# Both products with v of a round side by side, the scores laid out anew over five PSUM banks

## The chip, the cores and the metric

One Trainium2 chip, one of its cores. The metric is the device time of one execution in microseconds, as the median of several runs. A profile of one further execution gives the span from the first to the last instruction.

## What is computed

A gate mixes two branches over the same x (2048 positions, 640 features): a Fourier mix A and an attention B with 32 heads of 20 features that share one k and one v.

```python
g = sigmoid((x * gate_w).sum(-1, keepdims=True))
# A: a = x @ hid_re.T ; b = x @ hid_im.T ; y = seq_re @ a - seq_im @ b
# B: q = x @ wq per head ; k = x @ wk ; v = x @ wv
#    o = softmax(q k^T * 20**-0.5) v ; B = o @ wo
out = g * A + (1 - g) * B
```

All is float32. The large products use a float32r high part and a low part, three products for one.

## The kernel before

The first 266 us make q, k, v and the gate, then a and b of the Fourier branch. From there on a long stage runs two streams interleaved on TensorE (PE), which an order written out by hand sets: for ScalarE, VectorE, GpSimd and PE the instructions run as the program issues them.

*Attention.* The heads are taken in 16 pairs. Head 0 of a pair lies in partitions 0 to 63 and head 1 in 64 to 127, so a score product fills one half of PE's rows and two of them, one on each half, run beside each other. There are two kinds of scores. A unit `a` (`a_unit`, L319) multiplies a block of 128 queries by 512 keys and VectorE reduces it to its row maximum (L326). It works some 12 units ahead, mostly for the pair to come. A unit `b` (`b_unit`, L647) multiplies 128 keys by 512 queries, with the maximum in two extra rows, and ScalarE writes the exponential to an SBUF tile `pt` (L655). The products with v (`av_step`, L659) take four `pt` tiles, 128 keys deep, and write four groups of 32 columns of one bank: 128x32 tiles of PE, plain float32. Sixteen of them add up in a bank, and `finish_half` copies it out.

*Fourier.* The products `y` (L551) fill half of PE's rows as well, 320 columns wide, with one accumulating bank for each half (F0, F1). `y_evict` has ScalarE copy them out once 48 products a half are through.

A **round** issues 12 y on each half, 4 b and 4 a for each head, and two V, each an `av_step` on tiles of the round before. The string `ROUND` is its order, and `ROUND_LAST` that of the last pair's 16 rounds, which have no a. In these strings `y0` is a y on half 0, `a1S0` a score a of head 1 into bank S0, `b0S2` a score b of head 0 into bank S2, `V` an `av_step`, `E0` an eviction of y. Eight PSUM banks serve it: F0 and F1 for y, one bank V for the products with v, and S0 to S4 for the scores. A bank takes its next score when VectorE or ScalarE has read the last one; PE's weight load for that score carries the wait.

The last pair's products with v are laid out otherwise before: `av_half` splits the 128 keys into two halves of PE's rows (64x32 tiles, L676), `W0` and `W1` in the order, into two banks, V and S4; `finish_half` copies both (L691, L692) and GpSimd adds them (L693). After the 16 pairs 32 groups of products with wo (`o_group`, L114 to L116) end the kernel, and behind the first of them the last products with v run.

`clock` and `tick` count pairs of a (of b in the last pair). `a_reduce` (L332) runs one tick after a pair's last a, `a_final` (L340) three, and `finish_sums` (L716) 24 ticks after a pair's sums are out.

Of the kernel before, what the change touches and what calls it, by code (L numbers as in the profile page):

```python
# [8 lines left out]
F32 = mybir.dt.float32  # L9
F32R = mybir.dt.float32r  # L10
AF = mybir.ActivationFunctionType
ALU = mybir.AluOpType
# [5 lines left out]
P = 128  # L18
# [5 lines left out]
NT = S // P  # L24
NPAIR = H // 2
LAST = NPAIR - 1
# [3 lines left out]
ROW = 512  # L30
# [3 lines left out]
def kernel(  # L34
# [13 lines left out]
    nc = tc.nc  # L48
# [43 lines left out]
    vsb = const.tile([P, NT, 32], F32, name="vsb")  # L92
# [12 lines left out]
    def move(dst, src):  # L105
        nc.sync.dma_start(words(dst), words(src))  # L106
# [13 lines left out]
    RG = (slice(0, P // 2), slice(P // 2, P))  # L120
# [247 lines left out]
    def a_half(hh, tag="A"):  # L368
        u = state[hh]
        if u >= NA:  # L370
            return
        a_unit(u, hh, tag)
        state[hh] = u + 1
        if state[1 - hh] <= u:
            return
        if u % 64 == 16 and u // 64 + 1 < NPAIR:
            load_qs(u // 64 + 1)
        if u % 64 == 63:
            later(1, a_reduce, u // 64)
            later(3, a_final, u // 64)  # L380
# [35 lines left out]
    for it, t in enumerate(T2):  # L416
        load_x2(it + 2)
        j = t % SJ
# [37 lines left out]
    op = ctx.enter_context(tc.tile_pool(name="op", bufs=2))  # L456
# [113 lines left out]
    def y_evict(g):  # L570

        if not ended:
            return
        grp = ended[0]
        if "t" not in grp:
            grp["t"] = [op.tile([P, HALF], F32, name=n) for n in ("yt", "yu")]
            grp["left"] = 2
        y_half(g, grp["t"], grp["tb"], grp["ps"])
        grp["left"] -= 1
        if grp["left"] == 0:  # L580
            ended.pop(0)
            y_sum(grp["sh"], grp["tb"], grp["e"], grp["t"], grp["y0"])
# [53 lines left out]
    def y_put(n):  # L636

        while n > 0:
            n -= next(ys)[1]

    av = {}
    pt = {}

    def b_unit(p, hh, kc, qc, tag="B"):
        b = 64 * hh
        ps = bank(tag, f"b_{p}_{kc}_{qc}_{hh}")
        nc.tensor.matmul(  # L647
            ps,
            ks[b : b + 62, kc * P : (kc + 1) * P],
            qs[p][b : b + 62, qc * ROW : (qc + 1) * ROW],  # L650
            start=True,
            stop=True,
        )
        t = pp.tile([P, ROW], F32, name="pt")
        nc.scalar.activation(t, ps, AF.Exp, scale=SCALE)  # L655
        pt[(hh, kc, qc)] = [t, 2 if p == LAST else 1]

    def av_mm(ps, g, t, kc, first, last):
        nc.tensor.matmul(ps[32 * g : 32 * g + 32, :], vsb[:, kc, :], t, start=first, stop=last)  # L659

    def av_step(p, qh, kc):
        if kc == 0:
            av[qh] = bank("V", f"av_{p}_{qh}")
        for hh in range(2):
            for j in range(2):
                av_mm(av[qh], 2 * hh + j, pt.pop((hh, kc, 2 * qh + j))[0], kc, kc == 0, kc == NT - 1)

    avh = {}

    def av_half(g, p, qh, kc):  # L670

        if kc == 0:
            avh[g] = bank(("V", "S4")[g], f"av_{p}_{qh}_{g}")
        for i in range(4):
            key = (i // 2, kc, 2 * qh + i % 2)
            nc.tensor.matmul(  # L676
                avh[g][32 * i : 32 * i + 32],
                vsb[RG[g], kc, :],
                pt[key][0][RG[g]],
                start=kc == 0,  # L680
                stop=kc == NT - 1,
            )
            pt[key][1] -= 1
            if pt[key][1] == 0:
                pt.pop(key)

    def finish_half(p, qh):
        ob = op.tile([P, ROW], F32, name="ob")
        if p == LAST:
            oc = op.tile([P, ROW], F32, name="oc")  # L690
            nc.scalar.activation(ob, avh[0], AF.Copy)  # L691
            nc.scalar.activation(oc, avh[1], AF.Copy)  # L692
            nc.gpsimd.tensor_tensor(ob, ob, oc, op=ALU.add)  # L693
        else:
            nc.scalar.activation(ob, av[qh], AF.Copy)
        for hh in range(2):
            h = 2 * p + hh
            for j in range(2):
                js = slice((2 * qh + j) * ROW, (2 * qh + j + 1) * ROW)
                g = 32 * (2 * hh + j)  # L700
                move(sum_d[h : h + 1, js], ob[g + DH : g + DH + 1])
                move(oT_d[h * DH : (h + 1) * DH, js], ob[g : g + DH])
        if p == LAST:
            sm = op.tile([P, 16], F32, name="sm")
            ts = slice(qh * S // 2, (qh + 1) * S // 2)
            for hh in range(2):
                move(sm[64 * hh : 64 * hh + 64], sum_d[2 * p + hh, ts].rearrange("(s t) -> s t", t=16))
            later(4, finish_last, ts, sm)
        elif qh == 1:
# [14 lines left out]
    def finish_last(ts, sm):  # L724
# [10 lines left out]


    ROUND = (
        "y0 y1 y0 a1S0 b0S2 y1 b1S3 y0 y0 y1 y0 y1 y0 a1S1 y0 b0S4 y1 y1 y0 y1 y0 y1 y0 y1 "
        "a0S2 y1 y1 b0S3 a1S0 y0 y0 y1 b1S1 E1 a0S4 V a0S3 a1S0 E0 b0S1 b1S2 V b1S1 a0S4"
    ).split()  # L740

    ROUND_LAST = (
        "b1S3 y0 y1 y1 y0 y1 y0 b0S1 y1 y1 y0 b1S2 y0 y0 y1 y1 y0 y0 y1 y0 y1 y1 y0 b0S3 b1S0  "
        "y1 y0 y1 E1 y0 E0 b1S1 b0S2 W0 W1 W0 W1 b0S0"
    ).split()
    YR = ROUND.count("y0")
    ROUNDS = [(p, qh, kk) for p in range(NPAIR) for qh in range(2) for kk in range(NT // 2)]
# [5 lines left out]
        7: (lambda: [load_y(tb) for tb in range(4)],),  # L753
    }
    old = []
    old_h = [[], []]

    def av_next(g):
        if old_h[g]:
            st = old_h[g].pop(0)  # L760
            av_half(g, *st)
            if st[2] == NT - 1 and st not in old_h[1 - g]:
                finish_half(*st[:2])

    for rnd in ROUNDS:
        p, qh, kk = rnd
        nb, na, fed = [0, 0], 0, False
        new = [(p, qh, 2 * kk), (p, qh, 2 * kk + 1)]
        plan = ROUND
        if p == LAST:  # L770
            plan = ROUND_LAST

            if rnd[1:] == (0, 0):
                plan = ["V" if w == "W0" else w for w in plan if w != "W1"]
        for what in plan:
            if what == "V":
                if old:
                    st = old.pop(0)
                    av_step(*st)
                    if st[2] == NT - 1:  # L780
                        finish_half(*st[:2])
                continue
            g = int(what[1])
            if what[0] == "y":
                if not fed:
                    y_put(YR)
                    fed = True
                halves.run(g)
            elif what[0] == "E":
                y_evict(g)  # L790
            elif what[0] == "W":
                av_next(g)
            elif what[0] == "b":
                b_unit(p, g, 2 * kk + nb[g] // 2, 2 * qh + nb[g] % 2, what[2:])
                if p == LAST and sum(nb) % 2 == 0:
                    tick()
                nb[g] += 1
            else:
                if na % 2 == 0:
                    tick()  # L800
                a_half(g, what[2:])
                na += 1
        if p < LAST:
            old += new
        for g in range(2):
            old_h[g] += new if p == LAST else []
        if p == LAST and qh == 1:
            for f in BEFORE.get(kk, ()):
                f()
# [6 lines left out]
    for i in range(2 * NT):  # L816
        tb, e = divmod(i, 2)
        o_group(tb, e)
        tick()
        if i == 0:  # L820
            for g in (0, 1, 0, 1):
                av_next(g)
        n, k = divmod(i, 4)
        if k == 1:
            mult_o(n + 2)
        elif k == 2:
            split_o(n + 2)
            load_o(n + 3 if n else NO)
        if e == 1:
            load_y(tb + 4)  # L830
# [47 lines left out]
```

## Time and profile before

| | |
|---|---|
| time, median of 3 runs | 1862.59 us (1862.51 to 1863.89) |
| the profiled execution, span of its instructions | 1860.4 us |
| PE, weight loads, VectorE, ScalarE, GpSimd busy | 99%, 66%, 78%, 68%, 21% of the span |
| scores a and b, 512 columns | 2048 of each |
| y products, 320 columns | 6144 |
| records of products with v | 3840 (L659) and 512 (L676) |
| HBM traffic | 82 GB/s over the span |

Each float32 product with v shows as two records, so an `av_step` is eight records and two V of a round are sixteen. In a timeline's row stand the start in us from the span's start, the duration, the engine (PEld is the loading of weights on PE), the line, the operation, its tiles and shape, and how many records were merged; in brackets the idle time of the engine ahead of it and what ended that. In the list of waits the columns are the total in us, how often, and the longest.

### The profile page before, as it was taken

How to read it: one execution, taken by the hardware profiler on the slowest of the kernel's cores; microseconds unless marked ns; L12 is line 12 of the kernel's file. 1: busy time of each engine (PE TensorE's matmuls, PEld its weight loads, DVE VectorE, ACT ScalarE, POOL GpSimd, SP SyncE). 2: the span in 40 equal slices, each digit the busy share in tenths (PEclk: the TensorE clock that was granted, in tenths of full speed). 3: DMA queues.
4: the chain of work that ended last, by engine and by line, in shares of the span. 5: the costliest groups of instructions: out<-in, count | busy, mean ns of one | idle time of the engine just before them, and what ended most of it. 6: DMA issues, size and time to landing. Idle time of an engine off the chain costs nothing.

```text
span 1860.4 us, 42326 instructions
## 1 busy us (share of the span) xinstructions
PE 1846.3 (99%) x17368; PEld 1228.9 (66%) x17368; DVE 1449.3 (78%) x2307; ACT 1269.3 (68%) x2425; POOL 391.9 (21%) x336
## 2 busy tenths in 40 slices
PE   8999999999999999999999999999999999999999
PEld 6799986566566656656655665665566566566689
DVE  4469988888888888888888888888888888883144
ACT  4333357777777777777777777777777777778830
POOL 0033431111111111111111222222222212221132
PEclk9999999999999999999999999999999999999999
DMA  7684111211112021212114412121212121111366
GB/s 246 180 262 169 42 37 41 58 42 49 51 33 67 26 61 30 57 33 63 37 56 156 172 50 64 49 65 49 64 49 61 46 65 49 44 49 39 94 203 231
DMA packets 89023, 150.64 MB, mean 81 GB/s; under 512 B 21620, under 2 KB 58484, under 8 KB 86308
## 3 DMA queue, kind: packets, MB, share of 16 engines
q1 hardware_dynamic: 88828, 147.93, 25.8%
q8 instruction: 136, 2.23, 0.5%
q14 instruction: 59, 0.48, 0.1%
HBM read 103.91 MB, written 48.23 MB: 82 GB/s over the span
## 4 chain that ended last, share of the span: by engine, by line
PE 96%; DMA 2%; SPq 1%; DVE 1%; ACT 0%; issue 0%; POOL 0%; ACTq 0%; DVEq 0%
PE av L659 26%; PE y L551 23%; PE b L647 16%; PE a L319 16%; PE ab L125 7%; PE av L676 2%; PE o L114 1%; PE o L116 1%; PE o L115 1%; SPq L106 1%; PE q L116 1%; PE q L114 1%; PE q L115 0%; DMA ql_d<-ql 0%; DMA wraw<-in_wiT_dram 0%; DMA wraw<-in_wrT_dram 0%
## 5 line engine op out<-in xcount | busy, mean ns | idle before, releaser
L326 DVE TENSOR_REDUCE mx<-a 128x1 f32<-128x512 f32 x2048 | 1316.3, 686 | 217.1 <-PE a L319 124.3
L655 ACT ACTIVATE pt<-b 128x512 f32<-128x512 f32 x2048 | 1099.7, 599 | 358.6 <-PE b L647 352.5
L319 PE MATMUL a<-ks,qs 60*128 60x512 f32 x2048 | 755.8, 430 | 0.2 <-ACT pt L655 0.2
L551 PE MATMUL y<-ab,ch 64*128 64x320 f32 x4096 | 688.2, 307 | 1.2 <-DVE both L441 1.2
L647 PE MATMUL b<-qs,ks 62*128 62x512 f32 x2048 | 685.2, 407 | 0.7 <-ACT pt L655 0.7
L551 PEld LDWEIGHTS y<-ab,ch 64*128 64x128 f32 x4096 | 569.5, 186 | 12.8 <-DVE both L441 1.5
L659 PE MATMUL av<-pt,vsb 128*32 128x512 f32 x3840 | 511.3, 605 | 0.0
L647 PEld LDWEIGHTS b<-qs,ks 62*128 62x128 f32 x2048 | 331.8, 187 | 219.0 <-ACT pt L655 218.2
L319 PEld LDWEIGHTS a<-ks,qs 60*128 60x128 f32 x2048 | 335.0, 184 | 198.9 <-ACT pt L655 198.2
L551 PE MATMUL y<-ab,cl 64*128 64x320 f32 x2048 | 456.0, 308 | 0.0
L551 PEld LDWEIGHTS y<-ab,cl 64*128 64x128 f32 x2048 | 347.1, 187 | 0.8
L659 PEld LDWEIGHTS av<-pt,vsb 128*32 128x32 f32 x3840 | 76.0, 108 | 154.8 <-issue 146.5
L561 POOL TENSOR_TENSOR yt<-yt,yu 128x320 f32<-128x320 f32 x64 | 56.8, 888 | 575.6 <-ACT yt L556 563.2
L397 POOL CAST ch<-craw 128x1024 fp32r<-128x1024 f32 x62 | 64.4, 1039 | 477.1 <-PE a L319 441.3
L398 POOL TENSOR_TENSOR cl<-craw,ch 128x1024 fp32r<-128x1024 f32 x62 | 147.7, 2383 | 5.0
L125 PE MATMUL ab<-wh,xh 64*128 64x320 f32 x640 | 134.6, 308 | 1.5 <-DVE gz L235 1.1
L125 PE MATMUL ab<-wl,xh 64*128 64x320 f32 x640 | 134.1, 306 | 0.0
L125 PE MATMUL ab<-wh,xl 64*128 64x320 f32 x640 | 133.8, 306 | 0.0
L410 POOL TENSOR_TENSOR ab<-both,ab 128x320 fp32r<-128x320 f32 x64 | 60.3, 948 | 189.5 <-DMA craw<-in_cre_dram 99.9
L125 PEld LDWEIGHTS ab<-wh,xl 64*128 64x128 f32 x640 | 96.4, 185 | 0.0
L125 PEld LDWEIGHTS ab<-wl,xh 64*128 64x128 f32 x640 | 96.2, 185 | 0.0
L440 ACT ACTIVATE half<-ab 128x320 f32<-128x320 f32 x64 | 28.0, 437 | 88.4 <-PE ab L125 88.4
(86 smaller groups left out, 967.3 us busy)
## 6 DMA issues: line engine op xcount, KB each, us to landing
craw<-in_cre_dram SPq DMA_DIRECT2D x32, 512.0 KB
craw<-in_cim_dram SPq DMA_DIRECT2D x32, 512.0 KB
qs<-qh_d SPq DMA_DIRECT2D x64, 160.0 KB
ab_d<-ab SPq DMA_DIRECT2D x16, 640.0 KB
y_d<-yt SPq DMA_DIRECT2D x64, 160.0 KB
ab<-ab_d SPq DMA_DIRECT2D x16, 640.0 KB
xr<-in_xT_dram SPq DMA_DIRECT2D x20, 256.0 KB
xr<-in_xT_dram SPq DMA_DIRECT2D x16, 320.0 KB
```

The source lines that it names most:

```text
L114: nc.tensor.matmul(ps, wh, xh, start=(i == 0), stop=False)
L125: nc.tensor.matmul(ps, w[r], x[r], start=(i == 0 and k == 0), stop=(i == n - 1 and k == 2))
L319: nc.tensor.matmul(ps, qs[p][b : b + 60, qb * P : (qb + 1) * P], ks[b : b + 60, c * ROW : (c + 1) * ROW], start=True, stop=True,)
L326: nc.vector.tensor_reduce(mx[p][:, hh, qb, c : c + 1], ps, axis=AX.X, op=ALU.max)
L397: eng.tensor_copy(h, raw)
L398: eng.tensor_tensor(l, raw, h.bitcast(F32), op=ALU.subtract)
L410: nc.gpsimd.tensor_tensor(lo, both, hi.bitcast(F32), op=ALU.subtract)
L551: nc.tensor.matmul(ps, w, x, start=start, stop=stop)
L561: nc.gpsimd.tensor_tensor(yt, yt, yu, op=ALU.add)
L647: nc.tensor.matmul(ps, ks[b : b + 62, kc * P : (kc + 1) * P], qs[p][b : b + 62, qc * ROW : (qc + 1) * ROW], start=True, stop=True,)
L655: nc.scalar.activation(t, ps, AF.Exp, scale=SCALE)
L659: nc.tensor.matmul(ps[32 * g : 32 * g + 32, :], vsb[:, kc, :], t, start=first, stop=last)
```

## The change

`ROUND` and `ROUND_LAST` are written anew: the two V of a round stand side by side at its end, and y, a and b and their banks are spread otherwise. The counts of y, a, b, V and E in a round stay as they are, and so do each bank's (S0, S2, S3, S4 three times, S1 four times). The last pair uses `av_step` like the others; `av_half`, its second bank and the addition go away.

```diff
-        pt[(hh, kc, qc)] = [t, 2 if p == LAST else 1]
+        pt[(hh, kc, qc)] = t
...
-    def av_half(g, p, qh, kc):
...
     def finish_half(p, qh):
         ob = op.tile([P, ROW], F32, name="ob")
-        if p == LAST:
-            oc = op.tile([P, ROW], F32, name="oc")
-            nc.scalar.activation(ob, avh[0], AF.Copy)
-            nc.scalar.activation(oc, avh[1], AF.Copy)
-            nc.gpsimd.tensor_tensor(ob, ob, oc, op=ALU.add)
-        else:
-            nc.scalar.activation(ob, av[qh], AF.Copy)
+        nc.scalar.activation(ob, av[qh], AF.Copy)
...
     ROUND = (
-        "y0 y1 y0 a1S0 b0S2 y1 b1S3 y0 y0 y1 y0 y1 y0 a1S1 y0 b0S4 y1 y1 y0 y1 y0 y1 y0 y1 "
-        "a0S2 y1 y1 b0S3 a1S0 y0 y0 y1 b1S1 E1 a0S4 V a0S3 a1S0 E0 b0S1 b1S2 V b1S1 a0S4"
+        "a0S1 b1S0 b1S3 y0 y0 a1S2 y0 y1 y0 y1 b0S4 b1S0 a0S1 y1 y0 y1 y0 y1 y0 a1S3 b0S2 y0 y1 y0 y1 "
+        "a0S1 b1S4 y1 y0 y1 b0S0 y1 y0 y1 a1S2 y0 b0S3 y1 a1S4 a0S1 E0 E1 V V"
     ).split()
     ROUND_LAST = (
-        "b1S3 y0 y1 y1 y0 y1 y0 b0S1 y1 y1 y0 b1S2 y0 y0 y1 y1 y0 y0 y1 y0 y1 y1 y0 b0S3 b1S0  "
-        "y1 y0 y1 E1 y0 E0 b1S1 b0S2 W0 W1 W0 W1 b0S0"
+        "b1S3 b0S2 b1S0 y0 y0 y1 b0S4 y1 y1 y0 y1 y0 y1 b0S1 y1 y0 b1S3 y0 y1 y0 y1 y0 y1 y0 y1 y0 "
+        "y1 y0 y1 y0 b1S2 b0S0 E0 E1 V V"
     ).split()
...
-        if p < LAST:
-            old += new
-        for g in range(2):
-            old_h[g] += new if p == LAST else []
+        old += new
...
         if i == 0:
-            for g in (0, 1, 0, 1):
-                av_next(g)
+            for st in old:
+                av_step(*st)
+            finish_half(*old[-1][:2])
```

What PE gets at the end of a middle round before, in the order of issue. In these names `a_0_...` is a score a of head 0 with a running number, `b_11_3_0_...` a score b of key block 11, query block 3, head 0; `x4` is one V.

```order
L319 MATMUL a_0_5211<-ks,qs_867 128x512
L659 MATMUL av_1_4834<-pt,vsb 32x512 x4
L319 MATMUL a_0_5218<-ks,qs_867 128x512
L319 MATMUL a_1_5221<-ks,qs_867 128x512
L647 MATMUL b_11_3_0_5224<-qs_865,ks 128x512
L647 MATMUL b_11_2_1_5228<-qs_865,ks 128x512
L659 MATMUL av_1_4834<-pt,vsb 32x512 x4
L647 MATMUL b_11_3_1_5236<-qs_865,ks 128x512
L319 MATMUL a_0_5240<-ks,qs_867 128x512
```

Four scores stand between the two V, two for each head. On PE at the same place now:

```order
L319 MATMUL a_1_5323<-ks,qs_867 128x512
L319 MATMUL a_0_5326<-ks,qs_867 128x512
L659 MATMUL av_1_4855<-pt,vsb 32x512 x8
L319 MATMUL a_0_5337<-ks,qs_867 128x512
L647 MATMUL b_14_2_1_5340<-qs_865,ks 128x512
```

Both V have become one run of eight; the scores that stood between them have moved into the rest of the round. On PE, what follows directly in the new order:

```order
L647 MATMUL b_14_3_1_5344<-qs_865,ks 128x512
L551 MATMUL y_1_1_0_5063<-ab_3153,ch 128x320 x2
L319 MATMUL a_1_5350<-ks,qs_867 128x512
L551 MATMUL y_1_1_0_5063<-ab_3153,cl 128x320
L551 MATMUL y_1_1_1_5064<-ab_3153,ch 128x320
L551 MATMUL y_1_1_0_5063<-ab_3346,ch 128x320
L551 MATMUL y_1_1_1_5064<-ab_3153,ch 128x320
L647 MATMUL b_14_2_0_5357<-qs_865,ks 128x512
L647 MATMUL b_15_2_1_5361<-qs_865,ks 128x512
L319 MATMUL a_0_5365<-ks,qs_867 128x512
```

The last row, `a_0_5365`, uses bank S1 again, which `a_0_5337` behind the V used, and `b_15_2_1_5361` uses S0 again after `b_14_2_1_5340`. In the last pair, PE's order at the end of a round before:

```order
L647 MATMUL b_1_3_1_27305<-qs_865,ks 128x512
L647 MATMUL b_1_2_0_27309<-qs_865,ks 128x512
L676 MATMUL av_0_0_26768<-pt,vsb 32x512 x4
L676 MATMUL av_0_1_26773<-pt,vsb 32x512 x4
L676 MATMUL av_0_0_26768<-pt,vsb 32x512 x4
L676 MATMUL av_0_1_26773<-pt,vsb 32x512 x4
L647 MATMUL b_1_3_0_27345<-qs_865,ks 128x512
L647 MATMUL b_2_2_1_27349<-qs_865,ks 128x512
```

And PE's order at the end of a round of the last pair now:

```order
L647 MATMUL b_11_1_1_27038<-qs_865,ks 128x512
L647 MATMUL b_11_1_0_27042<-qs_865,ks 128x512
L659 MATMUL av_0_26772<-pt,vsb 32x512 x8
L647 MATMUL b_12_0_1_27054<-qs_865,ks 128x512
L647 MATMUL b_12_0_0_27058<-qs_865,ks 128x512
```

The round's last b of head 0 has moved from behind the products with v to the place ahead of them.

More of the change, by code (lines that the diff above doesn't have):

```diff
@@ L665, in av_step @@
             for j in range(2):
-                av_mm(av[qh], 2 * hh + j, pt.pop((hh, kc, 2 * qh + j))[0], kc, kc == 0, kc == NT - 1)
-    avh = {}
-    def av_half(g, p, qh, kc):
[L672 to L685, printed above, removed]
+                av_mm(av[qh], 2 * hh + j, pt.pop((hh, kc, 2 * qh + j)), kc, kc == 0, kc == NT - 1)
     def finish_half(p, qh):
         ob = op.tile([P, ROW], F32, name="ob")
-        if p == LAST:
-            oc = op.tile([P, ROW], F32, name="oc")
-            nc.scalar.activation(ob, avh[0], AF.Copy)
-            nc.scalar.activation(oc, avh[1], AF.Copy)
-            nc.gpsimd.tensor_tensor(ob, ob, oc, op=ALU.add)
-        else:
-            nc.scalar.activation(ob, av[qh], AF.Copy)
+        nc.scalar.activation(ob, av[qh], AF.Copy)
         for hh in range(2):
@@ L755 @@
     old = []
[L756 to L763, printed above, removed]
     for rnd in ROUNDS:
@@ L771 @@
             plan = ROUND_LAST
-            if rnd[1:] == (0, 0):
-                plan = ["V" if w == "W0" else w for w in plan if w != "W1"]
         for what in plan:
@@ L790 @@
                 y_evict(g)
-            elif what[0] == "W":
-                av_next(g)
             elif what[0] == "b":
@@ L820 @@
         if i == 0:
-            for g in (0, 1, 0, 1):
-                av_next(g)
+            for st in old:
+                av_step(*st)
+            finish_half(*old[-1][:2])
         n, k = divmod(i, 4)
```

## The prediction

> **What bounds the kernel now.** I read the page first, then the list of waits over the long middle stage (270 to 1700 us), then that stage's timeline one round at a time, then the places where a round is laid out in another way.
>
> ```profile
> PE 1846.3 (99%) x17368; PEld 1228.9 (66%) x17368; DVE 1449.3 (78%) x2307; ACT 1269.3 (68%) x2425; POOL 391.9 (21%) x336
> ...
> L326 DVE TENSOR_REDUCE mx<-a 128x1 f32<-128x512 f32 x2048 | 1316.3, 686 | 217.1 <-PE a L319 124.3
> L655 ACT ACTIVATE pt<-b 128x512 f32<-128x512 f32 x2048 | 1099.7, 599 | 358.6 <-PE b L647 352.5
> L319 PE MATMUL a<-ks,qs 60*128 60x512 f32 x2048 | 755.8, 430 | 0.2 <-ACT pt L655 0.2
> ...
> L659 PE MATMUL av<-pt,vsb 128*32 128x512 f32 x3840 | 511.3, 605 | 0.0
> ```
>
> PE is busy 99% of the span and the products wait for nothing worth naming (0.2 us before all of a). VectorE at 78% is next. In the middle stage the list of waits says the same:
>
> ```profile
> PEld b L647 <- ACT pt L655: 200.2, 239, 0.8
> PEld a L319 <- ACT pt L655: 196.9, 235, 0.8
> PEld av L659 <- issue: 144.8, 445, 0.4
> DVE mx L326 <- PE a L319: 115.0, 468, 0.4
> ```
>
> PEld loads weights ahead of the products. Its idle stretches come once per group of products with v (239 + 235 = 474, two for each round), and VectorE waits for PE. So PE's own sequence is the bound, and what counts is how long one round takes on it. One round:
>
> ```profile
> 905.56 0.39 PE L647 MATMUL b<-qs,ks 62*128 62x512 f32 x1
> 905.87 0.16 PEld L659 LDWEIGHTS av<-pt,vsb 128*32 128x32 f32 x8 [0.28 <-issue]
> 906.87 0.19 PEld L319 LDWEIGHTS a<-ks,qs 60*128 60x128 f32 x2 [0.84 <-ACT pt L655]
> 907.54 0.16 PEld L659 LDWEIGHTS av<-pt,vsb 128*32 128x32 f32 x8 [0.37 <-issue]
> 908.53 0.18 PEld L647 LDWEIGHTS b<-qs,ks 62*128 62x128 f32 x1 [0.84 <-ACT pt L655]
> ...
> 911.90 0.16 PEld L659 LDWEIGHTS av<-pt,vsb 128*32 128x32 f32 x8 [0.28 <-issue]
> ```
>
> From V to the same V is 6.03 us (905.87 to 911.90). Each V takes 1.00; between them stand four scores (0.67) and then the rest of the round (3.37). 2048 scores a, of which the earlier stage takes 152, make 237 such rounds: 1430 us of the span.
>
> **The change, part by part.**
>
> *Two V side by side.* This trace has one round where that already happens, the first of the last pair:
>
> ```profile
> 1705.99 0.40 PE L647 MATMUL b<-qs,ks 62*128 62x512 f32 x2
> 1706.32 0.16 PEld L659 LDWEIGHTS av<-pt,vsb 128*32 128x32 f32 x8 [0.28 <-issue]
> ...
> 1708.17 0.19 PEld L647 LDWEIGHTS b<-qs,ks 62*128 62x128 f32 x2 [0.84 <-ACT pt L655]
> ```
>
> Two V in a row take 1.85 (1706.32 to 1708.17) against 2 x 1.00. The second saving is one way in and out of the scores' shape. In the short block a half of the array runs two scores in 0.67. A score holds its half for 0.23 to 0.24, by the next two rows, which are one half's a and its next y:
>
> ```profile
> 909.03 0.40 PE L319 MATMUL a<-ks,qs 60*128 60x512 f32 x1
> ...
> 909.26 0.31 PE L551 MATMUL y<-ab,ch 64*128 64x320 f32 x1
> ```
>
> So a block costs 0.67 - 2 x 0.235 = 0.20 beyond its work, and the new round has one block fewer. If PE never waited, it would be 6.03 - 0.15 - 0.20 = 5.68 us, 237 x 0.35 = 83 us less. That is the gain on offer.
>
> The Trainium skill has the rule behind it, in TensorEngine Tiling (Array Packing), Key Properties: changing the tiling mode drains TensorE. The trace agrees: 0.15 and 0.20 us for one change of shape fewer. Going by that rule alone the kernel comes out near 1775, the second rival below. The same page, under PSUM Bottleneck, speaks against the change: tiling speeds up TensorE but not the emptying of PSUM. By that the gain ends where the score banks do, and this is what the next part finds from rows.
>
> *The new layout of the banks.* A bank can be written again only when its reader is through. The price of one such hand-over is in the trace in pieces. From the start of a late weight load to the reader:
>
> ```profile
> 906.87 0.50 PE L319 MATMUL a<-ks,qs 60*128 60x512 f32 x2
> ...
> 907.40 0.69 DVE L326 TENSOR_REDUCE mx<-a 128x1 f32<-128x512 f32 x1 [0.30 <-PE a L319]
> ```
>
> That is 0.53 to the reduction's start and 0.69 for the reduction. From a reader's end to the next weight load, for ScalarE and for VectorE:
>
> ```profile
> 1703.45 0.60 ACT L655 ACTIVATE pt<-b 128x512 f32<-128x512 f32 x1 [0.26 <-PE b L647]
> 1704.10 0.18 PEld L647 LDWEIGHTS b<-qs,ks 62*128 62x128 f32 x1 [0.27 <-ACT pt L655]
> 1704.10 0.49 PE L647 MATMUL b<-qs,ks 62*128 62x512 f32 x1
> ...
> 105.43 0.49 DVE L441 SCALAR_TENSOR_TENSOR both<-ab,half 128x320 f32<-128x320 f32 x1 [3.33 <-POOL ab L410]
> 105.97 0.18 PEld L125 LDWEIGHTS ab<-wh,xh 64*128 64x128 f32 x1 [0.59 <-DVE both L441]
> ```
>
> Both give 0.05, and the product behind a late load takes 0.49 again (0.40 where its weights were loaded ahead). So a bank used by a after a costs 0.53 + 0.69 + 0.05 = 1.27 us from weight load to weight load, and by b after b 0.10 less. A whole link of the latter stands in the trace and confirms the sum:
>
> ```profile
> 261.66 0.19 PEld L647 LDWEIGHTS b<-qs,ks 62*128 62x128 f32 x2
> 262.84 0.18 PEld L647 LDWEIGHTS b<-qs,ks 62*128 62x128 f32 x1 [0.99 <-ACT pt L655]
> ```
>
> 1.18 us. With the third decimals unknown I take 1.28 for the link of a, with 1.26 to 1.31 as its ends.
>
> Now the plans. Before, no bank comes back so soon: S1 from b0S1 to b1S1 is the shortest, with half the short block and a V between (0.67/2 + 1.00 = 1.33), and the waits above show no stall. After, S1 is used by head 0's a alone, four times in a round: right behind the two V, behind b0S4 b1S0, ahead of b1S4, and last. Half 0 has this to do from the first use to the second: a0 (0.235 + 0.10, its weights being late), four y (0.147 each, what 3.37 leaves for 12 y beside 6 scores and the 0.20) and b0 (0.235), 1.16 in all. From the second to the third it is a0, five y and b0, 1.21, and from the third to the last a0, three y and two b0, 1.15. The link wants 1.28 each time. So the four uses form a chain of three links, one behind the other, and the last of them stands just ahead of the V. From a late last score to the V:
>
> ```profile
> 1710.92 0.18 PEld L647 LDWEIGHTS b<-qs,ks 62*128 62x128 f32 x1
> ...
> 1711.34 0.11 PEld L676 LDWEIGHTS av<-pt,vsb 64*32 64x32 f32 x2 [0.24 <-PE b L647]
> ```
>
> 0.42. The round is then 3 x 1.28 + 0.42 + 1.85 = 6.11 us. PE's work without waits (5.68) fits inside, and so PE idles 0.43 in each round.
>
> I followed the other users through this round, counted from the end of the two V. b1S0 waits for its own S0 (1.18 us, just ahead of the S1 wait, so hidden). VectorE's four reductions start at 0.53, 1.14, 1.81 and 2.42 (0.61 apart when they queue), and the third a0S1 is ready at 3.09 when the engine is free at 3.03: no addition. The last three run on under the V and end at about 5.8, before the next a0S1 at 6.11. ScalarE's eight exponentials and the two y evictions behind them end before that too. The new pairing of E0 E1 ahead of the V is therefore free.
>
> Against 6.03 that is +0.08 a round, 237 x 0.08 = **+19 us**. Its ends: link 1.26 gives 6.05 (+5 us), 1.31 gives 6.20 (+40).
>
> *Small reductions in VectorE's queue.* Three further operations go through it for each of 15 pairs:
>
> ```profile
> L332 DVE TENSOR_REDUCE mxr<-mx x16: 285/286/287, 235.2 to 1688.3; 128x32 f32<-128x128 f32 x16
> ...
> L340 DVE STREAM_TRANSPOSE mt<-mxr x16: 200/202/213, 238.7 to 1688.7; 128x32 f32<-128x32 f32 x16
> ...
> L716 DVE RECIPROCAL rc<-sm x15: 341/344/346, 395.0 to 1742.6; 128x32 f32<-128x32 f32 x15
> ```
>
> Before, the slack of the banks hid them. After, by the ticks, the first falls into VectorE's pause behind the V (free), the transpose ahead of the third a0S1's reduction (0.06 of slack, so about 0.14 on the chain), the reciprocal among the last three (about 0.1 of the next round). 15 x 0.24 = **+3 us**, between 0 and 12 (all of the 0.83 each time).
>
> *Rounds without a.* Three rounds at the end of the middle stage: the S0 links of b come earlier without the scores a between. **0 to +1 us**, I take 0.5.
>
> *The last pair.* Its products with v in 64x32 tiles:
>
> ```profile
> 1702.91 0.18 PEld L647 LDWEIGHTS b<-qs,ks 62*128 62x128 f32 x1 [0.84 <-ACT pt L655]
> ...
> 1776.33 0.18 PEld L676 LDWEIGHTS av<-pt,vsb 64*32 64x32 f32 x16 [0.24 <-issue]
> ...
> 1778.21 0.19 PEld L647 LDWEIGHTS b<-qs,ks 62*128 62x128 f32 x2 [0.84 <-ACT pt L655]
> ...
> 1781.28 0.18 PEld L676 LDWEIGHTS av<-pt,vsb 64*32 64x32 f32 x16 [0.25 <-issue]
> ...
> 1783.16 0.18 PEld L647 LDWEIGHTS b<-qs,ks 62*128 62x128 f32 x1 [0.84 <-ACT pt L655]
> 1784.34 0.19 PEld L114 LDWEIGHTS o<-wo,qs 128*128 128x128 f32 x1 [0.99 <-ACT pt L655]
> ```
>
> All four take 1.88 where two V take 1.85: the tile shape itself is worth 0.03. The rest of a round is 3.07. New: 12 y and 4 scores a half, 12 x 0.147 + 4 x 0.235 + 0.20 = 2.90, and no bank comes back within 1.2 us, so 4.75 instead of 4.95. Sixteen rounds with the end of the stage: the last V of the pair before ends at 1702.91, the first o starts at 1784.34, 81.4 us; new 16 x 4.75 = 76.0. **-5.4 us**. 1.18 of it is the wait of o for the lone b0S0 that stood behind the V (1783.16 to 1784.34), which the new plan puts ahead of them. That finish_half loses a copy and an addition shortens a chain that PE does not wait for: 0.
>
> *Sum.* 19 + 3 + 0.5 - 5.4 = +17 us on the profiled span of 1860.4, so 1877.5. The runs' median of 1862.59 lies 2.2 us above that span, the launch around it; I add it: **1879.5 us**.
>
> **The rivals.**
>
> 1. *The S1 chain binds (my forecast)*: 1879, by itself 1867 to 1894. For it: each piece of the link is a row, and b's link stands whole. Against it: no row shows four a on one bank.
>
> 2. *PE is through with its stalls and only the changes of shape count.* Round 5.68: 1862.6 - 83 - 5 = 1775. It decides if a link costs at most (5.68 - 1.85 - 0.42)/3 = 1.14, which needs the 0.05 and most of the late load's 0.1 to vanish. The row of 1.18 for b, plus a reduction that is 0.09 longer than an exponential, speaks against it.
>
> 3. *A shorter link*, 1.14 to 1.24, because the other half of the array covers part of the late load: rounds of 5.7 to 6.0, 1778 to 1850. The late b at 1710.92 ran beside a busy half and still took 0.42 to the V against 0.33 after an early one (1705.99 to 1706.32), so the 0.1 is paid.
>
> 4. *Nothing to measure*: link 1.25 to 1.26, where the main rounds' -3 to +5 us and the other terms' -2 nearly cancel: 1858 to 1866.
>
> 5. *VectorE as a second queue*: some reductions start later after a V (908.53 to 909.11 in other rounds is 0.58 and not 0.53) and each link grows by 0.03 to 0.04: round 6.2, 1895 to 1905.
>
> **How the numbers follow.** Within 0.2% (3.7 us) counts as unchanged, about what a measurement of this kernel can tell. The forecast has 0.68, rival 5 0.08, rival 4 0.06, rival 3 0.10, rival 2 0.08. Faster is 2 and 3 together, 0.18; the same 0.06; slower 0.76. The likeliest's own range is 1867 to 1894. To leave out no more than 0.2 the range starts at 1856, in the upper end of rival 3 and with rival 4 inside, and ends at 1894.
>
> **What would show it.** Right: the time from two V to two V is 6.1 us, with 1.85 for the pair; weight loads of a (and of b at the second S0) with idle time ahead of them that ends with a reduction, two or three in a round; VectorE idle about 0.9 us once in a round; the last pair at 4.75; o's first wait gone. Wrong: a round near 5.7 without waits of PE's weight loads, or a pair of V above 1.85. If the forecast fails, it is by the link, three of which stand in each of 237 rounds: 0.01 us in a link is 7 us in the time.

## The result, and the profile after

The changed kernel takes 1882.96 us (median, 1881.66 to 1883.52) against 1862.64 us (1862.51 to 1863.89) for the kernel before beside it: a ratio of 1.0105, 95% interval 1.0090 to 1.0119. The forecast was 1879.0, with a range of 1856 to 1894. The profiled execution spans 1881.3 us against 1860.4, 20.9 more.

The page of the changed kernel has the engines and the costliest groups like this (columns: busy time, mean ns of one, idle time just before them and what ended most of it):

```profile
PE 1866.5 (99%) x17112; PEld 1294.4 (69%) x17112; DVE 1447.9 (77%) x2307; ACT 1226.5 (65%) x2423; POOL 389.4 (21%) x334
...
L326 DVE TENSOR_REDUCE mx<-a 128x1 f32<-128x512 f32 x2048 | 1318.3, 687 | 237.4 <-PE b L647 116.2
L655 ACT ACTIVATE pt<-b 128x512 f32<-128x512 f32 x2048 | 1056.2, 603 | 377.3 <-PE b L647 226.8
...
L319 PE MATMUL a<-ks,qs 60*128 60x512 f32 x2048 | 796.0, 440 | 2.0 <-DVE mx L326 1.6
...
L319 PEld LDWEIGHTS a<-ks,qs 60*128 60x128 f32 x2048 | 347.5, 184 | 241.8 <-DVE mx L326 190.6
L659 PE MATMUL av<-pt,vsb 128*32 128x512 f32 x4096 | 492.5, 598 | 0.0
```

PE shows 99% busy as before, VectorE 77% and ScalarE 65%. By these shares nothing has happened, and the kernel is 20 us slower. The share cannot show the loss: the record of a score (0.39 us) is longer than the 0.235 for which it holds its half, and behind a late load it is longer still (0.49 to 0.50; the mean of a rose from 430 to 440 ns), so the records cover short stalls. The list of waits of the changed kernel, 270 to 1700 us (total in us, how often, the longest):

```profile
PEld av L659 <- issue: 190.1, 673, 0.3
PEld a L319 <- DVE mx L326: 186.9, 223, 0.8
...
DVE mx L326 <- PE b L647: 114.9, 140, 0.9
DVE mx L326 <- PE a L319: 77.0, 96, 0.9
PEld b L647 <- ACT pt L655: 52.4, 233, 0.3
```

Before, no row had weight loads waiting for VectorE; now loads of a do, once a round. This row is easily misread. Its 0.84 us each time is the idle stretch of the weight loads behind the V, which the kernel before has too, there under ScalarE's name, and which stays 0.84 with the readers halved (below), there under "issue" (the profile shows nothing that the engine waited for). So the totals of this list do not show the chain. The distances between the loads into one bank do. One round, from the timeline of the weight loads:

```profile
907.43 0.16 PEld L659 LDWEIGHTS av<-pt,vsb 128*32 128x32 f32 x8 [0.24 <-PE y L551]
...
909.28 0.18 PEld L319 LDWEIGHTS a<-ks,qs 60*128 60x128 f32 x1 [0.84 <-DVE mx L326]
...
910.50 0.18 PEld L647 LDWEIGHTS b<-qs,ks 62*128 62x128 f32 x1 [0.22 <-ACT pt L655]
910.57 0.18 PEld L319 LDWEIGHTS a<-ks,qs 60*128 60x128 f32 x1
...
911.84 0.18 PEld L319 LDWEIGHTS a<-ks,qs 60*128 60x128 f32 x1
...
913.06 0.24 PEld L319 LDWEIGHTS a<-ks,qs 60*128 60x128 f32 x2
913.54 0.16 PEld L659 LDWEIGHTS av<-pt,vsb 128*32 128x32 f32 x8 [0.24 <-issue]
```

The four loads into S1 are at 909.28, 910.57, 911.84 and, as the second of the two merged at 913.06 (they end at 913.30, one takes 0.18), at 913.12. That is 1.29, 1.27 and 1.28 from one to the next. The pair of V takes 1.85 (907.43 to 909.28), the last use is followed by V after 0.42, and the round is 6.11. VectorE in the same round:

```profile
907.09 1.89 DVE L326 TENSOR_REDUCE mx<-a 128x1 f32<-128x512 f32 x3
909.82 4.07 DVE L326 TENSOR_REDUCE mx<-a 128x1 f32<-128x512 f32 x6 [0.85 <-PE a L319]
```

It stands still for 0.85 us under the V (its last reduction ended at 908.98, 0.30 ahead of the load at 909.28, which therefore did not wait for it) and begins 0.54 after the first load into S1, as the link has it. In the trace the reductions of the first three uses of S1 end at 910.51, 911.79 and 913.07, each 0.05 us ahead of the next load into S1. Each of the three links is thus made of the late product, its reader and the hand-over, with no other wait in it. Over 228 rounds the medians are 1.854 for the pair of V, 1.280, 1.281 and 1.280 for the links and 0.428 from the last load to the V, 6.12 together.

### The profile page after: what moved, and what is told of

The parts are those of the page before. It is cut to its first block, busy times and chain, and to the rows that moved or that the text cites. A ratio compares the mean times of both kernels' runs of the same rounds, so it can differ in the third digit from the quotient of the medians.

```text
span 1881.3 us, 41584 instructions
## 1 busy us (share of the span) xinstructions
PE 1866.5 (99%) x17112; PEld 1294.4 (69%) x17112; DVE 1447.9 (77%) x2307; ACT 1226.5 (65%) x2423; POOL 389.4 (21%) x334
## 3 DMA queue, kind: packets, MB, share of 16 engines
q1 hardware_dynamic: 88828, 147.93, 25.5%
## 4 chain that ended last, share of the span: by engine, by line
PE 96%; DMA 2%; DVE 1%; SPq 1%; ACT 1%; issue 0%; POOL 0%; ACTq 0%; DVEq 0%
PE av L659 26%; PE y L551 24%; PE b L647 17%; PE a L319 17%; PE ab L125 7%; PE o L114 1%; PE o L116 1%; PE o L115 1%; DMA ql_d<-ql 1%; SPq L106 1%; PE q L116 1%; PE q L114 0%; PE q L115 0%; DMA wraw<-in_wiT_dram 0%; DMA wraw<-in_wrT_dram 0%; DMA wraw<-in_wq_dram 0%
## 5 line engine op out<-in xcount | busy, mean ns | idle before, releaser
L655 ACT ACTIVATE pt<-b 128x512 f32<-128x512 f32 x2048 | 1056.2, 603 | 377.3 <-PE b L647 226.8
L647 PE MATMUL b<-qs,ks 62*128 62x512 f32 x2048 | 799.3, 430 | 1.7 <-ACT pt L655 1.4
L319 PE MATMUL a<-ks,qs 60*128 60x512 f32 x2048 | 796.0, 440 | 2.0 <-DVE mx L326 1.6
L551 PE MATMUL y<-ab,cl 64*128 64x320 f32 x2048 | 559.9, 308 | 0.0
L319 PEld LDWEIGHTS a<-ks,qs 60*128 60x128 f32 x2048 | 347.5, 184 | 241.8 <-DVE mx L326 190.6
L659 PE MATMUL av<-pt,vsb 128*32 128x512 f32 x4096 | 492.5, 598 | 0.0
L647 PEld LDWEIGHTS b<-qs,ks 62*128 62x128 f32 x2048 | 353.5, 185 | 78.8 <-ACT pt L655 70.3
L551 PEld LDWEIGHTS y<-ab,cl 64*128 64x128 f32 x2048 | 374.5, 187 | 4.4
L659 PEld LDWEIGHTS av<-pt,vsb 128*32 128x32 f32 x4096 | 106.8, 109 | 216.3 <-issue 208.7
L125 PE MATMUL ab<-wh,xh 64*128 64x320 f32 x640 | 133.7, 308 | 1.8 <-DVE gz L235 1.5
L125 PE MATMUL ab<-wl,xh 64*128 64x320 f32 x640 | 133.3, 306 | 0.0
L125 PE MATMUL ab<-wh,xl 64*128 64x320 f32 x640 | 133.0, 305 | 0.0
L125 PEld LDWEIGHTS ab<-wh,xl 64*128 64x128 f32 x640 | 96.3, 184 | 0.0
L125 PEld LDWEIGHTS ab<-wl,xh 64*128 64x128 f32 x640 | 96.2, 185 | 0.0
L125 PEld LDWEIGHTS ab<-wh,xh 64*128 64x128 f32 x640 | 84.5, 185 | 2.3 <-DVE gz L235 1.7
```

Of the source, the lines that this page charges most:

```text
L125: nc.tensor.matmul(ps, w[r], x[r], start=(i == 0 and k == 0), stop=(i == n - 1 and k == 2))
L319: nc.tensor.matmul(ps, qs[p][b : b + 60, qb * P : (qb + 1) * P], ks[b : b + 60, c * ROW : (c + 1) * ROW], start=True, stop=True,)
L551: nc.tensor.matmul(ps, w, x, start=start, stop=stop)
L647: nc.tensor.matmul(ps, ks[b : b + 62, kc * P : (kc + 1) * P], qs[p][b : b + 62, qc * ROW : (qc + 1) * ROW], start=True, stop=True,)
```

## The experiments

Each was compared with the kernel before on the same chip. First the times; the rounds are those of the middle stage, from V to the same V, as means over the rounds that have a:

| | time, us | ratio to before, 95% interval | round, us |
|---|---|---|---|
| changed kernel | 1882.96 | 1.0105 [1.0090, 1.0119] | 6.13 |
| last pair alone | 1857.82 | 0.9974 [0.9963, 0.9984] | 6.03 |
| one S1 use moved to S4 | 1875.37 | 1.0067 [1.0054, 1.0079] | 6.10 |
| V side by side, old banks | 1991.78 | 1.0689 [1.0675, 1.0704] | 6.57 |
| half reductions | 1844.80 | 0.9900 [0.9886, 0.9913] | 5.97 |
| half reductions and exponentials | 1781.95 | 0.9570 [0.9557, 0.9583] | 5.71 |
| the same halves in the kernel before | 1858.55 | 0.9981 [0.9972, 0.9990] | 6.03 |
| last pair, other split block | 1856.45 | 0.9969 [0.9957, 0.9980] | 6.03 |
| another plan, 16 tiles | 1873.77 | 1.0061 [1.0047, 1.0075] | 6.10 |
| another plan, 18 tiles | 1861.53 | 0.9994 [0.9985, 1.0002] | 6.04 |
| another plan, 21 tiles | 1861.61 | 0.9992 [0.9984, 1.0001] | 6.05 |
| another plan, 20 tiles | 1873.20 | 1.0054 [1.0041, 1.0068] | 6.09 |
| another plan, 6 and 12 tiles | 1848.22 | 0.9922 [0.9908, 0.9936] | 5.99 |

**One part alone.** The changed kernel with `ROUND` of before, so that only the last pair is new.

> The middle rounds in the old order, the last pair as changed. Chain theory (the +20 us sit in the 237 middle rounds, on bank S1): a round of the middle stays at 6.03 us, the last pair's rounds come to 4.75 and the first product with wo no longer waits, so -5 us against the kernel before: 1857. Rival, the loss sits in the last pair or the tail: slower than before, 1865 to 1883.

Measured 1857.82, 4.7 us less than before. The loss of the whole change therefore lies in the new `ROUND`: some 25 us (1882.96 - 1857.82).

**One use fewer on S1.** In the changed kernel the third a0 of the round goes to S4, and the b1 behind it to S1:

```diff
-        "a0S1 b1S4 y1 y0 y1 b0S0 y1 y0 y1 a1S2 y0 b0S3 y1 a1S4 a0S1 E0 E1 V V"
+        "a0S4 b1S1 y1 y0 y1 b0S0 y1 y0 y1 a1S2 y0 b0S3 y1 a1S4 a0S1 E0 E1 V V"
```

> The changed kernel with two letters exchanged: the third a0S1 writes S4 and b1S4 writes S1. Order, counts and the pair of V stay. Chain theory: the chain of four a on S1 is cut, the next longest hand-overs bind, a round comes to 6.05 us, 237 x 0.075 = 18 us less than the changed kernel: 1865. Rival, VectorE's total work or the pair of V itself makes the round 6.13: unchanged, 1883.

Measured 1875.37: the direction that the chain theory gives, but only 7.6 of its 18 us. Two rows, one round apart:

```profile
910.06 0.16 PEld L659 LDWEIGHTS av<-pt,vsb 128*32 128x32 f32 x8 [0.24 <-issue]
...
916.15 0.16 PEld L659 LDWEIGHTS av<-pt,vsb 128*32 128x32 f32 x8 [0.24 <-issue]
```

6.09 where 6.05 was expected. The expectation called the chain cut, and it is not: S1 still has four uses, the third of which is now a b. Over 229 rounds the medians of its links are 1.281, 1.279 and 1.243, so only the last became shorter, by 0.04 us. By the 1.18 that the trace before shows for b it should have been 0.10; the runs on another plan below show where such a difference can come from.

**V side by side without a new layout.** The kernel before, with its first V moved beside its second:

```diff
-        "... a0S4 V a0S3 a1S0 E0 b0S1 b1S2 V b1S1 a0S4"
+        "... a0S4 a0S3 a1S0 E0 b0S1 b1S2 V V b1S1 a0S4"
```

> The kernel before with its first V moved beside the second and nothing else: the old order and the old banks otherwise. Chain theory: eight scores now stand close together around the pair, their banks come back at once, a round comes to 6.57 us, 237 x 0.53 = 126 us more than before: 1988. Rival, only the changes of tile shape count: 0.35 less a round, 83 us less than before: 1780.

Measured 1991.78, a round of 6.57 as worked out:

```profile
964.12 0.18 PEld L319 LDWEIGHTS a<-ks,qs 60*128 60x128 f32 x1 [0.51 <-ACT pt L655]
964.59 0.18 PEld L319 LDWEIGHTS a<-ks,qs 60*128 60x128 f32 x1 [0.28 <-DVE mx L326]
...
965.25 0.16 PEld L659 LDWEIGHTS av<-pt,vsb 128*32 128x32 f32 x8 [0.36 <-issue]
...
971.81 0.16 PEld L659 LDWEIGHTS av<-pt,vsb 128*32 128x32 f32 x8 [0.37 <-issue]
```

Without the V between them the scores come back to their banks too soon, and the weight loads stand for ScalarE (0.51) and VectorE (0.28) just ahead of the V. So the first V in the middle of the short block did a job: it was the time in which banks came free. This costs 129 us; the new layout wins back 104 of them (1991.78 - 1882.96, less the 4.7 of the last pair).

**Shorter readers.** If the hand-over of banks eats the gain, then a kernel whose readers are short must show it. First VectorE alone, in the changed kernel; the maxima are taken over 256 of the 512 keys:

```diff
-        nc.vector.tensor_reduce(mx[p][:, hh, qb, c : c + 1], ps, axis=AX.X, op=ALU.max)
+        nc.vector.tensor_reduce(mx[p][:, hh, qb, c : c + 1], ps[:, : ROW // 2], axis=AX.X, op=ALU.max)
```

> The changed kernel with each row maximum taken over 256 of the 512 keys of a score (so the maximum of half the keys is subtracted). A reduction falls from 0.69 to about 0.42 us. Chain theory: the links of a on S1 shorten to about 1.0, the links of ScalarE's b on S0 (1.18) bind next, a round comes to 5.91 us: 1883 - 237 x 0.217 = 1831. Rival, VectorE's throughput is the bound: 2.1 us of its work go, PE's own 5.68 binds, 1777. Rival, the pair of V is dear in itself: unchanged, 1883.

Measured 1844.80, 38 us less than the changed kernel, between the 1831 of the chain theory and the 1883 of no change. In the list of waits the loads of a behind the V are still there, under another name (issue, 0.8 each). Those of b for the exponentials stay as they were:

```profile
DVE mx L326 <- PE a L319: 336.9, 580, 1.5
PEld a L319 <- issue: 174.4, 208, 0.8
...
PEld b L647 <- ACT pt L655: 54.0, 238, 0.4
```

Then both readers: the exponentials too go over 256 of 512 queries, into 16 fixed tiles whose other half holds a constant, so half of the attention is not computed. The same was done to the kernel before, as a control.

```diff
+    ptb = [pp.tile([P, ROW], F32, name=f"ptb{i}") for i in range(16)]
...
-        nc.scalar.activation(t, ps, AF.Exp, scale=SCALE)
+        nc.scalar.activation(t[:, : ROW // 2], ps[:, : ROW // 2], AF.Exp, scale=SCALE)
```

> The changed kernel with both readers of the score banks halved: row maxima over 256 of 512 keys, exponentials of 256 of 512 queries (the other half of each tile keeps a constant, so half of the attention's output is not computed). PE's instructions are the same. Chain theory: links of about 1.0 and 0.92 us no longer bind, a round comes to between 5.70 (PE's own work) and 5.77, so 1782 to 1798. Rival, the readers don't matter and the round is long by the pair of V: 1883.

> The kernel before with both readers halved in the same way (half of the attention's output is not computed). Chain theory: its rounds never waited for a bank, so they stay within 0.03 us of 6.03, and the last pair loses the 0.2 us a round that it waits for ScalarE: 1853 to 1861. Rival, VectorE and ScalarE hold up the kernel before as well: 1800 and less.

The changed kernel comes to 1781.95, a hundred us less; the kernel before to 1858.55, four less. A round with short readers (its lines are shifted, L664 is the product with v):

```profile
867.92 0.16 PEld L664 LDWEIGHTS av<-ptb,vsb 128*32 128x32 f32 x8 [0.29 <-issue]
...
869.78 0.18 PEld L319 LDWEIGHTS a<-ks,qs 60*128 60x128 f32 x1 [0.84 <-issue]
...
873.62 0.16 PEld L664 LDWEIGHTS av<-ptb,vsb 128*32 128x32 f32 x8 [0.28 <-issue]
```

5.70 us, where the prediction put PE's work without waits at 5.68. The gain on offer was there but for some hundredths of a us in a round, and the hand-over of banks took it. The kernel before has the same shortened work on both engines and hardly moves: it does all the work of VectorE and ScalarE within its 6.03 us, so the amount of that work is not what makes the round longer than that. The Trainium skill says in TensorEngine Tiling (Array Packing), PSUM Bottleneck, that tiling speeds up TensorE but not the emptying of PSUM. These two runs agree: the time saved on PE came out only when the readers were shortened.

**Another order inside the split block.** The last pair is new, `ROUND` is that of before, with E0 and a0S3 exchanged between the two V, which was to remove a delay of 0.04 us in the short block:

```diff
-        "... V a0S3 a1S0 E0 b0S1 b1S2 V b1S1 a0S4"
+        "... V E0 a1S0 a0S3 b0S1 b1S2 V b1S1 a0S4"
```

> The last pair as changed, the middle rounds in the old order with the two V apart, but with the eviction E0 ahead of the two scores a of the short block and those two exchanged. By following the round this takes away a delay of 0.04 us that the evictions bring in one round of four: 237 x 0.01 to 0.02, so 1852 to 1857. Rival, that delay is somewhere else: 1858 as with the old order.

Measured 1856.45. Its interval overlaps that of the last pair alone, so whether the exchange is worth anything stays open.

**Another plan for two V side by side.** The changed kernel with a `ROUND` in which no bank is used by a alone. Three of its hand-overs in a row go through S2 (`b1S2`, `a1S2`, `b0S2`, `a1S2`), two of them by the shorter exponential:

```diff
+        "a0S0 b1S2 a1S1 y0 b1S4 y0 y0 y1 y0 b0S3 y1 y1 y0 a1S2 b0S0 y1 y0 y1 a1S4 y0 b0S1 y1 y0 y1 "
+        "a0S3 y1 b0S2 y1 y1 y0 y1 y1 y0 E1 a0S0 b1S1 y0 b1S4 y0 a1S2 a0S3 E0 V V"
```

> The changed kernel with another order and other banks for the middle rounds, chosen by following a round with the durations of these traces: no bank is used twice by VectorE in close succession, the bank with four uses (S2) alternates b, a, b, a. The pair of V stays. Chain theory: 16 scores on 5 banks leave one bank with four uses and three hand-overs of 1.2 to 1.28 us between two pairs, so a round cannot go much below 6.00: with 6.00 to 6.03 it is 1849 to 1856. Rival, the pair of V costs more than the 1.85 once it stands in every round: 1870 and more. Rival, the changed kernel merely had a bad layout and a good one brings the whole gain: round 5.70, 1782.

Measured 1873.77: missed by 18 us. Weight loads, a product and an exponential of one round show where:

```profile
909.04 0.16 PEld L659 LDWEIGHTS av<-pt,vsb 128*32 128x32 f32 x8 [0.24 <-issue]
...
910.89 0.18 PEld L647 LDWEIGHTS b<-qs,ks 62*128 62x128 f32 x1
...
912.17 0.18 PEld L319 LDWEIGHTS a<-ks,qs 60*128 60x128 f32 x1
...
915.13 0.16 PEld L659 LDWEIGHTS av<-pt,vsb 128*32 128x32 f32 x8 [0.24 <-issue]
```

```profile
910.90 0.50 PE L647 MATMUL b<-qs,ks 62*128 62x512 f32 x1
```

```profile
911.52 1.09 ACT L655 ACTIVATE pt<-b 128x512 f32<-128x512 f32 x2 [1.87 <-PE b L647]
```

The product ends at 911.40 and its exponential, on an engine idle for 1.87 us, starts 0.12 later; so the first link is 1.28 us and not the 1.18 of b before. In the order, this exponential waits for two semaphores: PE's, and that of ScalarE itself, for the earlier writing of the same `pt` tile. In the trace such an exponential has a semaphore instruction of ScalarE's own ahead of it. The trace of the kernel before with halved readers has waiting exponentials of both kinds: the median from the product's end to the start is 0.037 us without it (965 of them) and 0.097 with it (490). That made 0.06 us a suspect, not yet a cause.

**Moving the second wait.** How many tiles the pool has decides which of a round's eight exponentials carry it, and nothing else in the order changes. By the order of issue, in the middle rounds (x carries it, q carries it in a quarter of the rounds):

```
tiles      b1S2 b1S4 b0S3 b0S0 b0S1 b0S2 b1S1 b1S4
16          x    q    .    .    x    x    .    x
18          x    q    x    x    .    .    .    x
21          .    q    x    x    x    x    .    .
20          x    q    x    x    x    x    .    .
6 and 12    .    q    x    .    x    .    .    x
```

The chain contains the two of S2. With 18 tiles the second of them is free of the wait, with 21 the first, with 20 neither.

```diff
-    pp = ctx.enter_context(tc.tile_pool(name="pp", bufs=16))
+    pp = ctx.enter_context(tc.tile_pool(name="pp", bufs=18))
```

> The new plan with 18 instead of 16 tiles for the exponentials; the order on every engine stays. By the order, this moves the second wait (on ScalarE's own earlier writing of the tile) among a round's eight exponentials: with 16 tiles the first and the sixth carry it, which are the two that read bank S2 ahead of a score a; with 18 the first carries it, the sixth no longer. If a second wait costs 0.06 us ahead of an exponential and the S2 chain sets the round, the round falls from 6.096 to about 6.05 and the time from 1873.8 by 11 to 14 us to 1860 to 1863. Rival, the round is set by something else: 1873 to 1875.

> The new plan with 21 tiles for the exponentials. Now the first exponential of a round carries no second wait, the sixth does. Second-wait theory: the round falls by 0.06 to about 6.04 and the time to 1859 to 1861. Rival, the round is set by something else: 1873 to 1875.

> The new plan with 20 tiles for the exponentials, as a control: the first and the sixth exponential both carry the second wait, as with 16 tiles; only others (third, fourth, seventh, eighth) change. Second-wait theory: no change, 1873 to 1875. Rival, more tiles help by themselves (an exponential that no longer waits for its tile): 1855 to 1865, as with 18 and 21.

Measured 1861.53, 1861.61 and 1873.20. Either removal brings 12 us (0.05 us in each of 237 rounds), the control with more tiles but both waits brings nothing. At the first exponential of a round, the median from its product's end to its start is 0.129 us with 16, 18 and 20 tiles, which leave the wait there, and 0.069 with 21, which take it away. In the lists of waits the row of the kernel with 20 tiles

```profile
PEld a L319 <- ACT pt L655: 44.0, 234, 0.5
```

has gone to

```profile
PEld a L319 <- ACT pt L655: 1.6, 6, 0.4
```

with 18, where the freed exponential is the one ahead of the last a1S2. Last, both removed at once, by a pool of 6 tiles for bank S2 and one of 12 for the rest:

```diff
-        t = pp.tile([P, ROW], F32, name="pt")
+        t = (pq if tag == "S2" else pp).tile([P, ROW], F32, name="pt")
```

> The new plan, with the tiles for exponentials from two pools: 6 tiles for the exponentials of bank S2 (the first and the sixth of a round), 12 for the other six. By the order neither of the first and the sixth carries the second wait any more. If each of them is worth about 12 us, as the runs with 18 and with 21 tiles showed one by one, both bring the new plan from 1873 to 1849 to 1852 (a round of 6.00), under the kernel before and under the version with the new last pair alone (1856 to 1858). Rival, behind the removed one another chain of 6.03 to 6.04 sets the round, and the second removal brings nothing: 1859 to 1862.

Measured 1848.22. The two removals add up (25.5 us). With 18 tiles the fifth exponential had lost the wait too, and with 21 the last; here both keep it, so it is the two of S2 that count. This version beats the kernel before by 0.78% and the changed kernel by 34.7 us. Its first link, and the exponential in it (lines shifted by one):

```profile
904.56 0.18 PEld L648 LDWEIGHTS b<-qs,ks 62*128 62x128 f32 x1
...
905.77 0.18 PEld L319 LDWEIGHTS a<-ks,qs 60*128 60x128 f32 x1
```

```profile
905.12 0.60 ACT L656 ACTIVATE pt<-b 128x512 f32<-128x512 f32 x1 [1.10 <-PE b L648]
```

1.21 instead of 1.28; the exponential starts 0.56 after the load, where with the second wait it was 0.63 (910.89 to 911.52). So the miss is explained, and by a cause that was switched on and off.

## Why the prediction was right

*Its parts.* The span can be cut at four places that both traces have: the end of the stage's first V group, the end of the last one ahead of the last pair's own rounds, and o's first weight load. The rows of the kernel before not shown so far, and those of the changed one:

```profile
267.87 0.16 PEld L659 LDWEIGHTS av<-pt,vsb 128*32 128x32 f32 x8 [0.37 <-issue]
...
268.87 0.18 PEld L647 LDWEIGHTS b<-qs,ks 62*128 62x128 f32 x1 [0.84 <-ACT pt L655]
```

```profile
259.67 0.18 PEld L647 LDWEIGHTS b<-qs,ks 62*128 62x128 f32 x1 [1.70 <-ACT pt L655]
...
260.50 0.33 PEld L647 LDWEIGHTS b<-qs,ks 62*128 62x128 f32 x1
...
265.70 0.18 PEld L319 LDWEIGHTS a<-ks,qs 60*128 60x128 f32 x1 [1.95 <-DVE mx L326]
...
271.82 0.18 PEld L319 LDWEIGHTS a<-ks,qs 60*128 60x128 f32 x1 [0.84 <-DVE mx L326]
...
1728.66 0.29 PEld L647 LDWEIGHTS b<-qs,ks 62*128 62x128 f32 x3 [0.84 <-ACT yu L556]
...
1779.44 0.16 PEld L659 LDWEIGHTS av<-pt,vsb 128*32 128x32 f32 x8 [0.28 <-issue]
...
1784.18 0.16 PEld L659 LDWEIGHTS av<-pt,vsb 128*32 128x32 f32 x8 [0.28 <-issue]
...
1805.24 0.19 PEld L114 LDWEIGHTS o<-wo,qs 128*128 128x128 f32 x1 [0.84 <-ACT pt L655]
```

| | before | after | difference | predicted |
|---|---|---|---|---|
| up to the end of the first V group | 268.87 | 271.82 | +2.95 | 0 |
| from there to 1702.91 / 1728.66 | 1434.04 | 1456.84 | +22.8 | +22.5 (19 + 3 + 0.5) |
| from there to o's first load | 81.43 | 76.58 | -4.85 | -5.4 |
| the rest | 76.06 | 76.06 | 0 | 0 |
| the span | 1860.4 | 1881.3 | +20.9 | +17.1 |

- *The pair of V, 1.85*: measured 1.85. The copy from the last pair of the trace before was the right row to take.
- *The S1 chain, a link of 1.28 and a round of 6.11*: links of 1.27 to 1.29, a round of 6.11 in the rows above, and 6.125 as the median of all. With half readers the chain is gone and the round is at 5.70. One working beside it was off: half 0's own work from the second to the third use was put at 1.21 without the 0.10 of a late product, which the working of the first use has. With it this work is 1.31, as long as the link; the median of that link is still 1.281.
- *Small reductions in VectorE's queue, +3, and the rounds without a, +0.5*: the middle stage as a whole came within 0.3 us of the three terms, but that is partly luck. The 235 rounds with a between the cuts grew by 0.092 in the median and not by 0.08, which is 21.6 us where 19 were forecast. The small operations are worth less than the forecast: the rounds with the reduction and the transpose take 6.145 in the median, 0.02 more than the others, and the second round behind each reciprocal takes 6.15; together this is under 1 us. Three rounds, 100 apart, take 6.25, by a third link of 1.41; none of them holds a small operation, and their cause is open. The rounds without a grew by 0.4.
- *The last pair, -5.4*: -4.85 here and -4.7 in the run of the last pair alone. Most rounds take the 4.75 that were worked out (1779.44 to 1784.18 is 4.74), but every fourth, with its evictions of y, takes 4.95; those were left out. o's first wait of 0.99 is 0.84 now, and the lone product ahead of it is gone.
- *What was overlooked* is the term of +2.95 at the entry of the stage. About half of it is waits: the weight loads stand idle for 0.78, 1.70, 1.95 and 0.23 us there, mostly on their banks' readers, against 1.45, 0.19, 0.51 and 0.99 before, 1.5 us more. The first round has no V, so no pause of 1.85 in which banks come free; that this is the reason was not tested. The other half is PE's clock. From 260.2 to 263.4 us the granted clock was 0.50 in this execution, and the loads take 0.33 us there instead of 0.18; before, it was 1.00 throughout. The run with one S1 use moved had 1.00 there as well, and came to the end of its first V group 14.4 us after the last product of the a and b branch (L125); the changed kernel took 15.9, the kernel before 13.1. The prediction followed the steady round alone.
- *Its signs in the profile*: VectorE idle 0.85 once a round (0.9 was given), the pair of V, the last pair and the size of the round were as said. "Two or three" waits of a's loads in a round do not appear as such: the list has 233 of b on ScalarE, one a round, and its 223 of a on VectorE are the pause under the V, which every version has. The S1 loads wait, by their distance of 1.28, but loads of y for the other half of PE fill that time, and the weight-load engine then isn't idle.

*The rivals.* Rival 2, that only the changes of shape count, had its condition named as a link of at most 1.14; with half readers it is what happens, and without them not. Rival 3 needed a link of 1.14 to 1.24, and rival 4 one of 1.25 to 1.26: neither is in the trace. Rival 5, VectorE as a second queue, wanted links of 1.31 and more, and they are 1.28: the 0.015 us between the median round of 6.125 and 6.11 is the third decimals of the pair and of the way from the last load to the V (1.854 and 0.428).

*What missed were three sizes in the experiments.* The new plan's was the second wait on ScalarE, shown above. The relief of S1 fell short by 10 us, because S1 kept its three links. The last of them, by an exponential, is 1.243 and not 1.18; this exponential carries a second wait and starts 0.097 after its product (median of 128). No run removed that wait, and by these rows it would not have brought the whole 0.06: the load into S4 beside it comes only 0.024 us earlier, straight behind its own reduction. The half reductions stayed 14 us above their expectation; halving the exponentials as well brought a further 63 us, so what was left lies in the banks that ScalarE reads, but in which of them was not tried. Whether 64x32 tiles cost more than 128x32 ones by themselves (1.88 against 1.85) was not tried either.

## What to carry to other kernels

A busy share of 99% with no waits ahead of the products does not mean that PE's work can be packed tighter: ask for each bank how many uses a round has and what one hand-over takes (here 1.2 to 1.3 us from weight load to weight load, four uses on one of five banks), and compare the sum with the round. Here three links, 0.42 and the pair of V make 6.1 us where PE's work alone is 5.7, so a saving of 0.35 us on PE turned into waits; the length of a link hangs on the engine that reads the bank between two uses and on the waits that this reader carries (1.28 by VectorE, 1.28 by ScalarE with a second wait at the first of a round's exponentials, 1.21 without it). To test such a claim cheaply, shorten the suspected readers in both kernels: the one that a chain binds moves (101 us here), the other hardly does (4 us, and its middle rounds stay at 6.03). An idle stretch in a list of waits is no proof of a chain, whatever it names as its end: the 0.84 us behind the V have the same length with long and with short readers.

## What the hardware showed beside that

- A second semaphore wait ahead of an instruction of ScalarE is not free. It starts 0.06 us later after its product's end (medians: 0.037 and 0.097 in the kernel before with halved readers, 0.069 and 0.129 at the first exponential of the new plan's round), and one such wait on the chain in each of 237 rounds is 12 us of the kernel. The number of buffers in a pool decides which instructions carry it: 18 and 21 tiles took 1861.5 us, 16 and 20 tiles 1873.
- Where two scores begin together on the two halves of PE, the exponential of the second starts some 0.03 us later: 0.069 after its product's end in the new plan without the second wait (904.56 + 0.50 to 905.12 in the rows above), against 0.037 for one whose product is the first or stands alone. No run exchanged the two.
- The granted clock fell to 0.50 for some 3 us at the entry of the middle stage in four profiled executions (the changed kernel, and the new plan with 16, 18 and 21 tiles) and stayed at 1.00 in the others. With 16 tiles the way from the last product of L125 to the end of the first V group took 14.7 us, with 20 tiles, in the same order and without the fall, 13.4.
